# State products of a gated linear attention on the four quarters of the matmul array, one PSUM bank per chunk

## Chip, cores and metric

One core of a Trainium2 chip. The metric is the device time of one execution in microseconds (us), as the median of a set's runs.

## The reference, cut to what matters

```python
# gateloop, B=4, H=8, S=768, D=48; then y is reshaped to (3072, 384) and goes through a maxout FFN
for t in range(S):
    new_re = ar * S_re - ai * S_im              # complex decay of the state
    new_im = ar * S_im + ai * S_re
    kv = np.einsum('bhd,bhe->bhde', k[:, :, t], v[:, :, t])
    S_re, S_im = (new_re + kv, new_im)
    y[:, :, t] = np.einsum('bhd,bhde->bhe', q[:, :, t], S_re)
h = np.maximum(np.maximum(x @ w1, x @ w2), x @ w3)   # 384 -> 768, three times
out = h @ w_out                                       # 768 -> 384
```

Everything is float32.

## The kernel before

A tile `x` is 128 tokens of one batch entry, made of two chunks of 64 tokens. There are 24 tiles; a group `g` is two of them. For each head, a tile needs the contribution of its tokens to the state, K^T V for each chunk ("dk"): 112 columns of the stationary operand (48 cosines in columns 0 to 47, 48 sines in columns 64 to 111, 16 zero columns between) times 48 values. The kernel did it with one matmul per head, for both chunks at once, by keeping v in a block-shaped buffer whose other half is zero:

```python
vbs = [const.tile([P, 2, H // 2, P], FP, ...)]   # [token, chunk, head pair, 2 x 48 (+32)]; token half h is loaded into chunk h, the rest stays 0

def both(t, h):                                  # a head's cosines and sines, 112 columns
    return t[:, h].rearrange("p u d -> p (u d)")[:, 0:DD]

def state(x):
    ...
    ps = psS.tile([P, 2, 512], FP, tag="s", name="dk")
    for h in range(H):
        o = h % 2 * (P - D)
        nc.tensor.matmul(out=ps[0:DD, h // HU, h % HU * 96:h % HU * 96 + 96],
                         lhsT=both(T["Uk", x], h),                  # 128 tokens x 112
                         rhs=T["v", x][:, :, h // 2, o:o + D], ...) # 128 tokens x (2 chunks x 48)
    dk = ps[0:DD, :, 0:HU * 96].rearrange("p a (b c d) -> p a b c d", b=HU, c=2)
    for c in ...:                                                   # VectorE: G_new = G * f + dk
        nc.vector.tensor_tensor(out=new, in0=heads(G[0:DD, c]), in1=f, op=OP.mult)
        nc.vector.tensor_tensor(out=new, in0=new, in1=dk[:, :, :, c], op=OP.add)
```

Other names in the profile: A and B are the score products (64 columns of weights, two column tiles), y the output products (32 columns, four column tiles), F the decay products (48 columns), tp transposes, up and op the FFN. The steps of the stages are listed in an order, and a scheduler then places each instruction on its engine:

```python
def tile_steps(x):
    tr, ct, pr = front(x + 1)          # tr: transposes, ct: F and its exponentials f, pr: VectorE products
    return [call(scores, x, "A"), call(gather, x, "A"), call(scores, x, "B")] + tr[:1] \
        + [call(gather, x, "B"), call(state, x)] + tr[1:] + ct + pr[:1] + kt \
        + [call(outputs, x, tokens(x))] + pr[1:]
```

In the first 113 us the float32 weights are also built from a wider stored form, a chain that goes back and forth between VectorE and ScalarE ("ex", "raw", "wo").

## Time and profile before

| | before |
|---|---|
| median | 742.48 us (742.40 to 744.02, 3 runs) |
| span of the profiled run | 740.5 us |
| TensorE busy | 91%, 7620 matmul records |
| VectorE, ScalarE busy | 70%, 54% |
| one dk stage in the steady part | 1.56 us, 24 of them in all |

The prediction below shows the lines. How to read them: a busy share is an average over stages, so it's cut into windows; the chain of work that ended last then tells, stage after stage, how long the next stage had to wait for this one. Matmul records come two per float32 matmul.

### The profile page before, as it was taken

To read this page: it belongs to the slowest core of one execution; us is meant where nothing else is said; L and a number is where in the kernel's file an instruction comes from. 1 tells how busy PE (TensorE), PEld (TensorE's weight loads), DVE (VectorE), ACT (ScalarE), POOL (GpSimd) and SP (SyncE) were. 2 spreads that over 40 slices of the span, in tenths; PEclk is the share of its full clock that TensorE was granted. 3 is DMA by queue.
4 is the path that set the end of the run, shared out by engine and by line. 5 is a ranking of instruction groups with operands and counts; after the bars stand their busy time and mean duration, and the time that the engine had idled before them with its cause. 6 is when DMAs were issued, how large, how long until landed. Compare 5 with 4: busy or idle time off the path is not lost.

```text
span 740.5 us, 17637 instructions
## 1 busy us (share of the span) xinstructions
PE 670.2 (91%) x7620; PEld 540.8 (73%) x7620; DVE 521.2 (70%) x718; ACT 400.8 (54%) x677; POOL 117.1 (16%) x121
## 2 busy tenths in 40 slices
PE   1266779789999999999999999999999999999998
PEld 0055668578778878878878778778778778778785
DVE  5999998897857867767757767767767677565210
ACT  6778655567556566466466466466475465322000
POOL 9200000403104004004005005004004004000000
PEclk9687799999999999999999999999999999999999
DMA  9780432140410410410410410410410210000000
GB/s 220 212 187 12 107 108 45 30 91 12 85 35 10 89 34 9 91 34 12 86 34 12 86 34 12 86 34 13 86 34 13 44 34 2 1 23 2 12 12 22
DMA packets 134158, 38.91 MB, mean 53 GB/s; under 512 B 126784, under 2 KB 129856, under 8 KB 134080
## 3 DMA queue, kind: packets, MB, share of 16 engines
q1 hardware_dynamic: 133824, 37.76, 23.0%
q8 instruction: 60, 0.98, 0.6%
q14 instruction: 18, 0.15, 0.1%
q10 hardware_dynamic: 256, 0.01, 0.0%
HBM read 33.03 MB, written 4.72 MB: 51 GB/s over the span
## 4 chain that ended last, share of the span: by engine, by line
PE 71%; issue 13%; DVE 7%; ACT 6%; DMA 1%; POOL 1%; SPq 0%; ACTq 0%; POOLq 0%; DVEq 0%
PE up L589 34%; PE op L600 12%; PE tp L442 5%; PE dk L539 4%; PE B L502 4%; PE y L567 3%; PE A L502 3%; ACT e L106 2%; PE mds L405 2%; PE cs L360 2%; PE sfx L405 2%; PE F L455 2%; ACT L L106 1%; ACT w L106 1%; PE cs L362 1%
## 5 line engine op out<-in xcount | busy, mean ns | idle before, releaser
L589 PE MATMUL up<-xT,w 128*128 128x256 f32 (+1 forms) x1404 | 297.5, 365 | 6.7 <-ACT xT L575 6.6
L589 PEld LDWEIGHTS up<-xT,w 128*128 128x128 f32 x1404 | 247.5, 190 | 46.2 <-ACT xT L575 8.9
L600 PE MATMUL op<-wo,hT 128*128 128x384 f32 x288 | 98.9, 492 | 7.3 <-DVE wo L292 3.9
L338 POOL TENSOR_TENSOR ai<-ai,L 128x768 f32<-128x768 f32 x10 | 25.8, 2578 | 382.4 <-ACT L L106 309.0
L600 PEld LDWEIGHTS op<-wo,hT 128*128 128x128 f32 x288 | 52.9, 191 | 41.5 <-issue 4.3
L594 DVE TENSOR_TENSOR hT<-hT,up 128x512 f32<-128x512 f32 (+1 forms) x78 | 49.8, 640 | 40.2 <-PE up L589 40.1
L469 DVE TENSOR_TENSOR Q<-Q,f 112x512 f32<-112x512 f32 x48 | 41.2, 857 | 42.0 <-ACT f L106 42.0
L444 ACT COPY K<-tp 112x512 f32<-112x512 f32 x48 | 27.9, 582 | 61.1 <-PE tp L442 61.0
L592 ACT COPY hT<-up 128x512 f32<-128x512 f32 (+1 forms) x39 | 21.4, 548 | 69.4 <-PE up L589 69.4
L602 ACT COPY ot<-op 128x384 f32<-128x384 f32 x24 | 11.5, 479 | 86.5 <-PE op L600 86.5
L551 DVE TENSOR_TENSOR g<-g,dk 112x384 f32<-112x384 f32 x40 | 22.1, 552 | 47.9 <-PE dk L539 47.4
L567 PEld LDWEIGHTS y<-atm,vb 128*32 128x32 f32 x1536 | 39.3, 111 | 13.9 <-issue 7.9
L539 PEld LDWEIGHTS dk<-vb,uk 128*112 128x112 f32 x384 | 42.0, 180 | 6.8 <-issue 2.5
L567 PE MATMUL y<-atm,vb 128*32 128x64 f32 x1536 | 46.6, 223 | 0.4 <-DVE atm L520 0.4
L567 PE MATMUL y<-QG,g 112*32 112x64 f32 x1536 | 46.0, 221 | 0.0
L469 DVE TENSOR_TENSOR QB<-Q,f 112x512 f32<-112x512 f32 (+1 forms) x48 | 45.4, 982 | 0.0
L539 PE MATMUL dk<-vb,uk 128*112 128x96 f32 x384 | 42.4, 264 | 3.1 <-issue 2.3
L502 PE MATMUL B<-QB,KB 112*64 112x96 f32 x768 | 37.8, 252 | 7.3 <-DVE QB L469 7.3
L502 PEld LDWEIGHTS B<-QB,KB 112*64 112x64 f32 x768 | 33.8, 140 | 11.5 <-issue 10.9
L405 PE MATMUL mds<-Ln,mid 128*128 128x384 f32 x48 | 23.9, 582 | 20.1 <-POOL cuts L120 15.9
L106 ACT ACTIVATE f<-F 48x296 f32<-48x296 f32 x96 | 39.6, 413 | 1.4 <-PE F L455 0.2
L502 PE MATMUL A<-Q,K 112*64 112x96 f32 x768 | 37.7, 249 | 2.6 <-DVE Q L469 2.4
(111 smaller groups left out, 1111.9 us busy)
## 6 DMA issues: line engine op xcount, KB each, us to landing
ar<-in_a_re_dram SPq DMA_DIRECT2D x24, 192.0 KB, 3.7
ai<-in_a_im_dram SPq DMA_DIRECT2D x24, 192.0 KB, 3.9
k<-in_k_dram SPq DMA_DIRECT2D x24, 192.0 KB, 2.9
q<-in_q_dram SPq DMA_DIRECT2D x24, 192.0 KB, 3.0
vb<-in_v_dram SPq DMA_DIRECT2D x96, 48.0 KB, 2.4
out_dram<-ot SPq DMA_DIRECT2D x24, 192.0 KB, 1.9
raw<-in_moe_w_dram SPq DMA_DIRECT2D x5, 768.0 KB, 6.5
raw<-in_moe_w_out_dram SPq DMA_DIRECT2D x3, 768.0 KB, 4.4
```

The costliest lines, as they stand in the source:

```text
L106: tab(nc.scalar.activation(**kw))
L338: (nc.gpsimd if g > 1 else nc.vector).tensor_tensor(out=ai, in0=ai, in1=L, op=OP.mult)
L405: nc.tensor.matmul(out=ps, lhsT=mat, rhs=T["Ln", g][:, c * DM:(c + 1) * DM], start=True, stop=True)
L442: nc.tensor.transpose(out=tp[0:DD, j], in_=both(T["U" + nm, x], hg * HU + j), identity=ident)
L444: nc.scalar.copy(out=T["K", x][0:DD, hs], in_=tp[0:DD])
L469: nc.vector.tensor_tensor(out=out, in0=in_, in1=f.to_broadcast([DD, H, 2 * n, 8]), op=OP.mult)
L502: nc.tensor.matmul(out=ps[o:o + L64, h // HU, h % HU * 96:h % HU * 96 + 96], lhsT=K[0:DD, h, o:o + L64], rhs=Q[0:DD, 2 * h + c], start=Tru ...
L539: nc.tensor.matmul(out=ps[0:DD, h // HU, h % HU * 96:h % HU * 96 + 96], lhsT=both(T["Uk", x], h), rhs=T["v", x][:, :, h // 2, o:o + D], st ...
L567: nc.tensor.matmul(out=y[32 * (r % 4):32 * (r % 4) + 32, r // 4, c * L64:(c + 1) * L64], lhsT=V[:, c, i, lo:lo + 32] if new else G[0:DD, c ...
L589: nc.tensor.matmul(out=ps[:, j], lhsT=ws[i][:, d, f * P:(f + 1) * P], rhs=xT[:, d], start=(d == 0), stop=(d == KD - 1))
L594: nc.vector.tensor_tensor(out=dst, in0=dst, in1=ps, op=OP.max)
L600: nc.tensor.matmul(out=ps, lhsT=hT[:, f, o:o + P], rhs=wo[:, f], start=(f == 0), stop=(f == KF - 1))
```

## The change

The intent: a product of two chunks in one matmul multiplies as many zeros as values. The array can act as four quarters of 64 rows by 64 columns. So a chunk's 64 tokens take half of the rows, a head's cosines or its sines half of the columns, and the four small products of a head run side by side. Each chunk gets its own PSUM bank; the prediction says why.

```diff
         for h in range(H):
             o = h % 2 * (P - D)
-            nc.tensor.matmul(out=ps[0:DD, h // HU, h % HU * 96:h % HU * 96 + 96],
-                             lhsT=both(T["Uk", x], h),
-                             rhs=T["v", x][:, :, h // 2, o:o + D], start=True, stop=True)
-        dk = ps[0:DD, :, 0:HU * 96].rearrange("p a (b c d) -> p a b c d", b=HU, c=2)
+            for lo, hi in ((0, L64), (L64, DD)):
+                for c in range(2):
+                    r = slice(c * L64, (c + 1) * L64)
+                    nc.tensor.matmul(out=ps[lo:hi, c, h * D:(h + 1) * D], lhsT=both(T["Uk", x], h)[r, lo:hi],
+                                     rhs=T["v", x][r, c, h // 2, o:o + D], start=True, stop=True)
+        dk = ps[0:DD, :, 0:DM].rearrange("p c (i u d) -> p c i u d", u=2, d=D)
 ...
-                nc.vector.tensor_copy(out=new, in_=dk[:, :, :, c])
+                nc.vector.tensor_copy(out=new, in_=dk[:, c])
 ...
-            nc.vector.tensor_tensor(out=new, in0=new, in1=dk[:, :, :, c], op=OP.add)
+            nc.vector.tensor_tensor(out=new, in0=new, in1=dk[:, c], op=OP.add)
```

## The prediction

> **What bounds the kernel now.** I read the page's busy shares first, then the table by windows, then the waits of TensorE alone, and last the chain of work that ended last. The shares say where to look, not what the bound is:
>
> ```profile
> PE 670.2 (91%) x7620; PEld 540.8 (73%) x7620; DVE 521.2 (70%) x718; ACT 400.8 (54%) x677; POOL 117.1 (16%) x121
> ```
>
> TensorE leads, but an average over 740 us hides stages, so I cut the span into windows. Columns of the table: the window, its length, busy time (instructions) of PE, PEld, DVE, ACT and POOL, then granted clock, DMA share and GB/s.
>
> ```profile
> 50.00:100.00 50.00, 35.69 (x426) 30.42 (x424) 48.01 (x73) 33.65 (x53) 1.03 (x1) 0.80 0.38 93
> 100.00:150.00 50.00, 41.33 (x571) 32.25 (x573) 42.34 (x59) 29.09 (x50) 8.97 (x6) 0.97 0.23 53
> ...
> 261.10:316.24 55.14, 54.33 (x629) 44.09 (x628) 40.17 (x52) 31.56 (x53) 9.57 (x6) 1.00 0.22 45
> ```
>
> There are two regimes. Until about 190 us VectorE is nearly full (48.0 of 50 us) while TensorE idles. From about 206 us the kernel repeats with a period of about 55.1 us, one group of two 128-token tiles each, and TensorE is busy for 54.3 us of it; VectorE has 15 us to spare, ScalarE 23. The waits of TensorE between 200 and 700 us confirm it (columns: total, times, longest, in us):
>
> ```profile
> PE up L589 <- ACT xT L575: 6.0, 8, 0.8
> PE A L502 <- issue: 0.2, 1, 0.2
> ```
>
> So in the steady part a microsecond taken from TensorE is a microsecond of time, once per tile. The chain of one such group (start, duration in us, line, instructions), where durations run from the end of one stage to the end of the next:
>
> ```profile
> 333.61 2.59 PE up L589 x12
> 336.20 1.56 PE dk L539 x16
> 337.76 2.62 PE up L589 x12
> ...
> 345.98 1.95 PE y L567 x116
> ...
> 361.06 1.47 PE A L502 x32
> 362.53 1.32 PE B L502 x32
> ```
>
> The reader should see the stage to be changed, dk, between two stages that use the whole array, and A, B and y, which already split it by columns. They are the only evidence in this profile of what a split costs and gains. The 1.56 us of dk is 16 instructions (8 heads, each fp32 matmul in two passes) at 97.5 ns. Streaming doesn't set that pace: up streams 256 columns in 2.59 us / 12 = 216 ns, or 0.84 ns a column, so dk's 96 columns need 81 ns. Its 112-column weight load does: 97.5 / 112 = 0.87 ns a column.
>
> **What the Trainium skill says.**
> - "TensorE: Matmul & The Clock Gate", section "LDWEIGHTS (loading the stationary operand)": the load takes columns / 1.2 ns, whatever the rows. For 112 columns that is 93 ns; the trace's 97.5 ns per pass agrees, about 4 ns over.
> - "TensorEngine Tiling (Array Packing)", section "Key Properties": tiles load and multiply in parallel, but changing the tiling mode drains the engine. Both are in the trace: A passes 32 instructions in 1.47 us, 46 ns each, half of one tile's 81 ns stream; and a switch costs time, worked out below.
> - "PSUM — Partial Sum Buffer", section "PSUM bank collisions raise a hardware error": tiles of different rows must not write one bank at once. This is why the change gives each chunk its own bank. No run so far has row tiles.
> - The first page again, section "Wait — 56ns, not 53.3ns?": start to start never below about 25 ns. The trace differs: y's chain entry counts 116 matmul records in 1.95 us; the code issues 128 (some records are missing), which makes 15.2 ns each over four column tiles. The measurement decides.
>
> **The change part by part.**
> *Removed:* per tile 8 matmuls (16 passes) of 128x112 weights by 96 columns, 1.56 us. Half of that product is wasted: each token half multiplies 48 columns of zeros in the block-shaped v.
> *Added:* per tile 32 matmuls (64 passes, 64 loads), each 64 rows by 64 or 48 weight columns by 48 moving columns. The four quarters of a head are issued in turn. If they run side by side, each quarter sees 16 passes. One pass there is the longer of its stream, 48 x 0.84 = 40 ns, and its load, 64 x 0.87 = 56 ns (42 ns for the 48-column quarter). So the load still binds: 16 x 56 = 0.90 us. The issue is a second bound nearby: 64 matmuls at y's 15.2 ns = 0.97 us. I take 0.94 us.
> *Added, hidden in the intent:* two mode switches per tile. The instruction order of both builds shows that in the steady part dk's neighbours don't change: op or up before, tp or up after, all full-array. Entering: A after up takes 1.47 us, the equal B right after A 1.32, so 0.15 us. Leaving: in the same chain up takes 2.79 us after B and 2.59 otherwise, 0.20 us; tp after B 1.02 against 0.87, 0.15 us. One visit thus costs 0.15 + (0.15 or 0.20), about 0.33 us.
> *Unchanged:* VectorE reads the same 112x384 values per half (552 ns each), now from one bank; transfers and evacuations are the same.
> *Sum per tile:* 0.94 + 0.33 = 1.27 us against 1.56 us plus the 0.03 us that up loses after dk on half of the visits, about 1.58: **0.31 us less**.
> *Where it counts:* the dk stages at 206 us and later, two in each of nine groups and one at 697.7 us, are 19. The first five, at 56, 96 to 98, 124, 152 and about 172 us, lie in the stretch whose chain runs through VectorE. There I count nothing. The new order even cuts some of the early stages up (one around an up step, one around transposes), which adds switches in time that TensorE has idle. 19 x 0.31 = 5.9 us. From 742.5 us that is **736.5 us**, 0.8% less.
>
> Does ScalarE take it back? In each group TensorE waits 0.8 us for the copy xT, at the end of a ScalarE stretch that starts when sfx has been multiplied (chain: 323.39 sfx, ScalarE 324.13 to 328.22). sfx comes after dk on TensorE, so that stretch starts earlier with it, and nothing else in it is new. I expect the 0.8 us to stay and the gain to pass through.
>
> **Rivals.**
> 1. *Quarters that differ in rows alone don't overlap*, so only two column tiles run side by side. Then 32 x 56 = 1.80 us + 0.33 = 2.13, 0.55 us more than now, 19 x 0.55 = +10 us: 753. For it: only column tiles are seen running together here. Against it: the skill's tiling page calls all tiles independent.
> 2. *Issue takes over.* With the skill's 25 ns floor, 64 x 25 = 1.6 + 0.33 = 1.93 us: 19 x 0.35 = +7 us: 749. Against it: y's 15.2 ns.
> 3. *The switch is cheaper or is hidden* by the row split, or loads of the two column widths decouple so that a pass costs nearer its stream. 0.90 us with no switch saves 0.68 x 19 = 13 us: 730. For it: nothing in this profile; A, F and y all show the switch.
> 4. *Another engine becomes the bound.* VectorE works 40 of 55 us, ScalarE 32; losing 0.6 us per group can't make them binding. It would give 742.
>
> **Range and chances.** My working gives 736.5. Between a pace of 50 ns a pass with 21 stages that count (saving 0.45 x 21 = 9 us) and 1.1 us a stage with 17 (0.15 x 17 = 2.5 us) lies 733 to 740; with the runs' own spread (742.4 to 744.0) and a little for rivals 1 and 2, I say 731.5 to 741.5. Over 2% faster means below 727.6 us, or 0.78 us less in each of 19 stages: more than rival 3 gives, 3%. Over 2% slower means above 757.3, 0.78 us more in each: more than rival 1, or quarters that hardly overlap: 4%. Within 2%: 93%.
>
> **What would show each step right or wrong.** In the profile after: dk should have 4 times the instructions (1536 matmul records in place of 384), and its chain entry should be about 1.05 to 1.15 us for 64 passes, the entry switch included; up after dk should rise from 2.62 to about 2.79, tp from 0.87 to about 1.02; the group's period should fall from 55.1 to about 54.5 us; the waits for xT should stay at 0.8 us. A dk entry near 2 us means rival 1, near 1.7 us rival 2, near 0.9 with up at 2.6 rival 3. If dk shrinks as said and the period doesn't, rival 4. The prediction is wrong if row tiles behave unlike column tiles, in load or in output, which no trace here shows.

## The result and the profile after

The changed kernel took 739.91 us (738.74 to 741.61, 4 runs) where the kernel before took 742.44 us (742.17 to 744.02, 4 runs). The ratio is 0.9963, with a 95% interval of 0.9939 to 0.9988. The gain is 0.4%, about 2.5 us, where 5.9 us had been forecast.

First the steady part, in the chain of the changed kernel (start, duration, line, instructions; some records are missing, so 57 or 58 stand for 64):

```profile
317.43 1.06 PE dk L544 x58
318.49 1.02 PE tp L442 x8
...
337.36 1.07 PE dk L544 x57
338.42 2.79 PE up L593 x12
```

The dk entry fell from 1.56 to 1.06 us, and the next stage pays for the switch back: 1.02 us for tp, 2.79 us for up. Those are the three figures that the prediction gave. From the first dk of the steady part to the last, 18 visits later, the chain of before goes from 205.96 to 697.68 us, 491.72 us; that of the changed kernel from 208.49 to 694.46 us, 485.97 us. That is 5.75 us, or 0.32 us a visit. Hardly anything took it back: TensorE's waits between 200 and 700 us add up to 6.6 us, where they were 6.2 us. One visit no longer waits for xT and waits 0.9 us at A instead; that group took 54.79 us, the others about 54.47 (columns: total, times, longest).

```profile
PE up L593 <- ACT xT L579: 5.7, 7, 0.8
PE A L502 <- issue: 0.9, 1, 0.9
```

So the steady part did what was forecast. But its first dk starts at 208.49 us, 2.53 us later than before. In this profile the loss is all ahead of the steady part. Following equal instructions of VectorE through both traces, they agree within 0.4 us up to about 107.5 us but for one stage that is ahead at 58 us; then one step of the weight chain comes 1.3 us late, and from 119 us on it's 2.5 to 2.7 us. Here is that place on ScalarE in the timeline of before (start, duration, engine, line, what, and in brackets the idle time ahead of it with what ended it):

```profile
106.72 0.94 ACT L285 ACTIVATE ex<-ex,biases 128x768 int32<-128x768 int32 x1 [1.85 <-DVE ex L284]
107.56 1.67 ACT L106 ACTIVATE f<-F 48x296 f32<-48x296 f32 x4
```

And in the changed kernel:

```profile
106.58 1.69 ACT L106 ACTIVATE f<-F 48x296 f32<-48x296 f32 x4 [1.82 <-PE F L455]
108.30 0.93 ACT L285 ACTIVATE ex<-ex,biases 128x768 int32<-128x768 int32 x1
```

The scheduler has turned two steps around: the four exponentials f, which need F from TensorE, now stand ahead of ex, which VectorE waits for. Nothing in the diff says so; a dk stage of another make-up in tile 1, ahead of this place, was enough (run only1 below). VectorE bounds this stretch, and its timeline shows the wait, first in before, then in the changed kernel:

```profile
107.94 0.95 DVE L286 SCALAR_TENSOR_TENSOR ex<-raw,ex 128x768 int32<-128x768 int32 x1
...
109.26 0.96 DVE L286 SCALAR_TENSOR_TENSOR ex<-raw,ex 128x768 int32<-128x768 int32 x1 [1.16 <-ACT ex L285]
```

The other 1.2 us come a little later. TensorE now waits 2.1 us for the first input of A (1.05 us before), and the step op behind that runs at a lowered clock: its first four matmul records take 2.93 us, where they took 1.56. Behind them is up, for which hT of VectorE then waits, again in before and in the changed kernel:

```profile
119.20 0.41 DVE L594 TENSOR_TENSOR hT<-hT,up 128x256 f32<-128x256 f32 x1
...
121.70 0.42 DVE L598 TENSOR_TENSOR hT<-hT,up 128x256 f32<-128x256 f32 x1 [1.13 <-PE up L593]
```

The window table, before and then changed (window, length, busy times of PE, PEld, DVE, ACT, POOL, then the granted clock as a mean over the window, DMA share and GB/s):

```profile
103.50:107.00 3.50, 3.41 (x21) 2.16 (x22) 3.49 (x6) 1.20 (x2) 0.00 (x0) 0.70 0.52 200
...
113.50:118.00 4.50, 4.36 (x37) 3.35 (x37) 4.50 (x5) 1.19 (x3) 0.00 (x0) 1.00 0.60 130
...
103.50:107.00 3.50, 3.50 (x21) 2.10 (x22) 3.29 (x6) 1.34 (x2) 0.00 (x0) 0.64 0.52 188
...
113.50:118.00 4.50, 4.24 (x28) 2.44 (x30) 4.50 (x6) 0.30 (x1) 0.00 (x0) 0.64 0.22 33
```

So the clock was 0.70 and 1.00 in before, 0.64 and 0.64 in the changed kernel.

### The profile page after: what moved, and what is told of

Its sections match the earlier page's. It is cut to its first block, busy times and chain, and to the rows that moved or that the text cites. A ratio compares the mean times of both kernels' runs of the same rounds, so it can differ in the third digit from the quotient of the medians.

```text
span 737.0 us, 19905 instructions
## 1 busy us (share of the span) xinstructions
PE 664.8 (90%) x8772; PEld 526.1 (71%) x8772; DVE 520.6 (71%) x718; ACT 401.4 (54%) x677; POOL 119.0 (16%) x121
## 3 DMA queue, kind: packets, MB, share of 16 engines
q8 instruction: 69, 1.13, 0.7%
## 4 chain that ended last, share of the span: by engine, by line
PE 69%; issue 17%; ACT 6%; DVE 5%; DMA 1%; POOL 1%; SPq 0%; POOLq 0%; ACTq 0%; DVEq 0%
PE up L593 33%; PE op L604 12%; PE tp L442 5%; PE B L502 4%; PE y L571 3%; PE dk L544 3%; PE A L502 2%; PE mds L405 2%; ACT e L106 2%; PE cs L360 2%; PE F L455 2%; PE sfx L405 2%; ACT L L106 1%; ACT w L106 1%; DMA w<-in_moe_w_dram 1%
## 5 line engine op out<-in xcount | busy, mean ns | idle before, releaser
L604 PE MATMUL op<-wo,hT 128*128 128x384 f32 x288 | 100.4, 498 | 6.6 <-DVE wo L292 3.9
L502 PEld LDWEIGHTS A<-Q,K 112*64 112x64 f32 x768 | 33.1, 138 | 11.2 <-issue 6.0
L571 PEld LDWEIGHTS y<-QG,g 112*32 112x32 f32 x1536 | 40.0, 111 | 0.5 <-issue 0.5
```

The lines of the kernel that those rows point to most:

```text
L502: nc.tensor.matmul(out=ps[o:o + L64, h // HU, h % HU * 96:h % HU * 96 + 96], lhsT=K[0:DD, h, o:o + L64], rhs=Q[0:DD, 2 * h + c], start=Tru ...
L571: nc.tensor.matmul(out=y[32 * (r % 4):32 * (r % 4) + 32, r // 4, c * L64:(c + 1) * L64], lhsT=V[:, c, i, lo:lo + 32] if new else G[0:DD, c ...
L604: nc.tensor.matmul(out=ps, lhsT=hT[:, f, o:o + P], rhs=wo[:, f], start=(f == 0), stop=(f == KF - 1))
```

## The experiments

**Theory (start).** The quarters are worth what was forecast in the steady part. The early loss isn't theirs; it comes from the order on ScalarE that the scheduler picked once tile 1's dk looked different, and from the clock of TensorE. **Rivals:** the loss belongs to the quarters (extra mode switches, stages cut in two) and is spread over the kernel; or it is chance.

### Control: the changed kernel again

> Control, the changed kernel unaltered, in the same rounds as the other three. Theory (start): the steady part gains 5.8 us as predicted (dk entries 1.06 us, period 54.5 us), and some 2.5 to 2.7 us are lost before 122 us, half of it because four exponentials of ScalarE now stand ahead of a weight-rounding step, half because the longer idle time of TensorE lets its clock fall to half for one op step. Then about 739.9 us again. Rival (chance): the first four runs were unlucky and the mean moves towards 737.

Measured: 739.96 us (6 runs, 738.22 to 741.48), ratio 0.9957 (0.9941 to 0.9973). The loss isn't bad luck of the first four runs.

### Quarters only where VectorE doesn't bound: late5

```diff
-        for h in range(H): ...quarters...
+        if x >= 5:
+            for h in range(H): ...quarters...
+        else:
+            for h in range(H): ...one matmul per head, as before...
```

The order of the steps of every engine is then that of before.

> Quarters in tiles 5 to 23 only, the old form in tiles 0 to 4; every engine's order is then that of the kernel before. Theory (start): nothing is lost early, the 19 steady stages gain 5.8 us: 736.6 us against 742.4. Rival (the loss belongs to the quarters themselves, spread over the kernel, or is chance): no better than the changed kernel, 739.9.

Measured: 736.13 us, ratio 0.9903 (0.9889 to 0.9917), against 0.9957 for the changed kernel in the same rounds. Five stages fewer are changed, and it's 4 us faster. In its chain the first steady dk starts at 206.20 us, as in before:

```profile
206.20 1.06 PE dk L545 x58
```

The last starts at 691.84 us, 485.64 us later. The rival that spreads the loss falls.

### Quarters in tile 1 alone: only1

```diff
+        if x == 1:
             ...quarters...
+        else:
+            ...as before...
```

> Quarters in tile 1 alone. Theory (start): this one stage is what reorders ScalarE; it saves a few tenths of TensorE time where TensorE is idle anyway, and costs 1.3 us for the order and up to 1.4 us more if the clock falls: 743.7 to 745.1 us. Rival (the order is harmless): 742.4 or a little less.

Measured: 747.42 us, ratio 1.0058 (1.0041 to 1.0075): 4 us slower than before, more than the 1.3 to 2.7 us expected. One stage of 24, which saves TensorE a few tenths of a microsecond, costs 4 us. The order of its ScalarE steps differs from before in just this place (f ahead of ex, and one copy K two places later), that of TensorE in one (y begun before op). In its profile TensorE's clock was 0.50 from 104 to 108 us and ex of VectorE started at 111.40 us after a wait of 2.30 us for ScalarE.

### The full change with one ordering edge: ordered

```diff
-        nc.scalar.activation(out=ex, in_=ex, func=AF.Relu, scale=8.0, bias=wbias)
+        T["rounding"] = nc.scalar.activation(out=ex, in_=ex, func=AF.Relu, scale=8.0, bias=wbias)
 ...
+                if x == 2:   # f of tile 2 stays behind the rounding step
+                    tc.add_manual_dep(ins.ins, T["rounding"].ins.name, order, reason="rounding first")
```

> The changed kernel in full, with one added ordering edge: the four exponentials f of tile 2 stay behind the rounding step ex on ScalarE, as before. Theory (start): the 1.3 us come back for certain, and with them the shorter idle time of TensorE, so that its clock stays up: 736.6 to 738.5 us. Rival (the loss comes from the extra mode switches and the split stages, which this kernel keeps): 739.9.

Measured: 735.75 us (5 runs, 734.81 to 736.48), a little below the expected range, ratio 0.9899 (0.9884 to 0.9914) against 0.9957 (0.9941 to 0.9973) for the changed kernel in the same rounds. All 24 stages keep their quarters, their extra switches and their cuts, and the loss is gone with one edge that isn't even waited for by a semaphore:

```profile
106.60 0.94 ACT L287 ACTIVATE ex<-ex,biases 128x768 int32<-128x768 int32 x1 [1.94 <-DVE ex L286]
107.44 1.67 ACT L106 ACTIVATE f<-F 48x296 f32<-48x296 f32 x4
...
107.82 0.95 DVE L288 SCALAR_TENSOR_TENSOR ex<-raw,ex 128x768 int32<-128x768 int32 x1
```

Compared step by step, the two traces have the same order on every engine, this one exchange apart. The changed kernel's other new places (y begun inside op at 108 us, one copy K of ScalarE at 101 us, a dk stage cut in three at 154 us, a few steps of VectorE, ScalarE and GpSimd between 125 and 145 us) are all still there, so they are not what cost the time; the exchange is. The gain of 1.0% is the forecast one and a little more.

### Columns alone and rows alone: cols5 and rows5

Both split tiles 5 to 23 only, so that the start stays as before. A second control went with them.

```diff
 # cols5: 128 rows, two column halves          # rows5: two row halves, 112 columns, a bank per chunk
-                for c in range(2): ...          -            for lo, hi in ((0, L64), (L64, DD)):
+  lhsT=both(T["Uk", x], h)[:, lo:hi]            +  lhsT=both(T["Uk", x], h)[r]
+  rhs=T["v", x][:, :, h // 2, o:o + D]          +  rhs=T["v", x][r, c, h // 2, o:o + D]
```

> Control in the same rounds as the next three: quarters in tiles 5 to 23, again about 0.990 of the kernel before, 736 us where that takes 743.

> As late5, but tiles 5 to 23 are split by columns alone: 32 passes of 128 rows, 96 moving columns with their zeros, two tiles side by side. Theory (a pass takes the longer of its stream and its load, tiles overlap, a visit costs two switches): 32 passes at 41 ns as in A, 1.32 + 0.15 us, so a dk entry of 1.47 us, the next up at 2.79 us; a visit costs 1.65 against 1.58 us: 19 x 0.07 = 1.3 us slower than before, about 744.5 where before takes 743. Rival (the column split alone carries the gain): as fast as late5.

> As late5, but split by rows alone: 32 passes of 64 rows, 112 weight columns, 48 moving columns, one bank per chunk. Theory: the 112-column load still takes 98 ns, two row tiles side by side, 16 x 98 = 1.57 + 0.15 us, a dk entry of 1.72 us; a visit costs 1.90 against 1.58: 19 x 0.32 = 6 us slower than before, 749 where before takes 743. Rival (row tiles don't load side by side): a dk entry of 3.3 us and some 773 us. Second rival (fewer rows load or stream faster): a dk entry below 1.56 us.

Measured: late5_again 737.43 us, ratio 0.9919 (0.9899 to 0.9938); cols5 743.44 us, 1.0002 (0.9984 to 1.0020), so in time no different from before; rows5 748.69 us, 1.0077 (1.0058 to 1.0096).

A warning from late5_again's profile. No step before its first steady dk differs from before, in form or in order, and yet that dk starts 2.71 us later than before's 205.96:

```profile
208.67 1.06 PE dk L545 x58
```

So the 2.53 us that the first two profiles showed lie within what single profiles of an unchanged start differ by. That the new order costs time rests on the sets of runs, and on the waits inside the traces, not on these two start times.

The chains, of cols5:

```profile
336.88 1.46 PE dk L543 x31
338.34 2.79 PE up L600 x12
```

and of rows5:

```profile
340.04 1.71 PE dk L544 x32
341.75 2.79 PE up L600 x12
```

Expected were 1.47 and 1.72 us. From the first to the last steady dk cols5 needs 492.82 us and rows5 497.18 us, against 491.72 of before: +0.06 and +0.30 us a visit, where +0.07 and +0.32 had been worked out. So the model of a pass holds for each half of the split by itself: columns alone shorten the load but leave the zeros to stream, rows alone drop the zeros but leave the 112-column load, and either pays the switches. Only both together win.

### One switch fewer: nextf5

```diff
-            + [call(gather, x, "B"), call(state, x)] + tr[1:] + ct + ...
+            + [call(gather, x, "B")] + tr[1:] + [call(state, x)] + ct + ...   # from tile 5 on
```

> As late5, but from tile 5 on dk is issued behind the second transposes, right ahead of F, which is split by columns too. Theory (each change of the array's mode costs 0.15 to 0.2 us, whatever the two modes): one visit to the full array between dk and F falls away in 18 tiles, 0.15 to 0.2 us each: 2.7 to 3.6 us less than late5, about 733 where late5 takes 736. Rival (a switch from one split to another costs as much as two, or the later G makes y wait): no gain over late5.

Measured: 733.03 us, ratio 0.9869 (0.9846 to 0.9891), against 0.9919 for late5_again in the same rounds: 0.5%, 3.7 us. The chain:

```profile
335.77 2.59 PE up L601 x12
338.37 1.07 PE dk L545 x57
339.43 0.65 PE F L455 x16
```

F takes 0.65 us behind dk as it did behind tp, so going from one split to another costs what going from the full array costs, no more. The switch back to the full array between them is gone: the chain from the first to the last steady dk is 481.78 us.

### The clock of TensorE: after_third, filled, best

One more control, a kernel that fills TensorE's second idle time, and one that joins what helped.

> Control, the changed kernel again in the same rounds: about 0.996 of the kernel before. In its profile the granted clock between 114 and 118 us is again near 0.6.

Measured: 737.66 us (735.94 to 739.06), ratio 0.9934 (0.9919 to 0.9948), better than the 0.996 that I had expected. And the profiled run, the fastest, contradicts what I expected of it. The order on ScalarE is the bad one, and yet little is lost:

```profile
105.16 1.69 ACT L106 ACTIVATE f<-F 48x296 f32<-48x296 f32 x4 [0.95 <-PE F L455]
106.88 0.94 ACT L285 ACTIVATE ex<-ex,biases 128x768 int32<-128x768 int32 x1
```

Here f started 1.4 us earlier than in the first profile, since F had run at full clock. The window table of this run has 1.00 where the first profile had 0.64:

```profile
103.50:107.00 3.50, 2.94 (x45) 1.46 (x44) 3.39 (x6) 2.49 (x6) 0.00 (x0) 1.00 0.34 135
```

VectorE's ex started at 107.84 us, about as in before. A part of that was luck: VectorE came to this place 0.55 us earlier than in before and lost 0.46 us of it here, waiting 0.37 us for ScalarE. So the theory needed one more part. The bad order makes ScalarE, and through it VectorE, wait for F; how long depends on the clock that TensorE happens to have there. It has just waited for a weight to be finished, in the timelines of before, of the changed kernel and of this third profile in turn:

```profile
103.59 1.61 PE L600 MATMUL op<-wo,hT 128*128 128x384 f32 x4 [3.85 <-DVE wo L292]
```
```profile
103.47 1.90 PE L604 MATMUL op<-wo,hT 128*128 128x384 f32 x4 [3.90 <-DVE wo L292]
```
```profile
102.94 1.53 PE L604 MATMUL op<-wo,hT 128*128 128x384 f32 x4 [3.50 <-DVE wo L292]
```

The Trainium skill, page "TensorE: Matmul & The Clock Gate", section "What's actually happening", says that the clock falls to half after at least one idle window of about 3.4 us, and that the window runs freely, so that where it falls differs from run to run. These waits are just on that edge, and the runs agree: after waits of 3.90, 4.13, 3.50 and 3.82 us the granted clock from 103.5 to 107 us was 0.64, 0.51, 1.00 and 0.66 in the four profiles of the changed kernel, and 0.70 in before after 3.85 us. The length alone doesn't decide: filled fell to 0.50 after 3.55 us, ordered kept 1.00 after 3.67 us. Before loses nothing there, because ex stood ahead of f. Nor do kernels that have its order or the mended one: nextf5 and best had clocks of 0.62 and 0.53 in this window, and their ex on VectorE started at 107.85 and 107.86 us.

> The changed kernel with two useless matmuls of 512 columns (1.7 us in all at full clock) in TensorE's idle time ahead of A of tile 2; ScalarE keeps the order f ahead of ex. Theory (two parts of the early loss): the granted clock stays at 1.0 in the op step behind, which gives back the 1.3 us that its halving cost and leaves the other 1.3 us: about 738.6 where the changed kernel takes 739.9. Rival (the clock falls with the longer wait as such, or the 1.3 us are hidden): the same as the changed kernel or slower by the filler's own time.

Measured: 738.53 us, ratio 0.9941 (0.9925 to 0.9956), no better than the control's 0.9934. In its profile the second fall of the clock is gone as intended (1.00 from 113.5 to 118 us), but the first stage was slow in that run (0.50, ex on VectorE at 110.43 us), and the filler takes its own time; two steps of VectorE also changed places. So its time tells nothing about the size of the second part. Its trace does, in the table under warm. For the larger loss I had filled the wrong gap.

> Everything that helped in one kernel: quarters in all tiles, the ordering edge for tile 2, and from tile 5 on dk right ahead of F. Theory: as fast as nextf5 or a few tenths faster, 0.986 to 0.987 of the kernel before: 732.5 to 733.5 where before takes 743.

Measured: 733.54 us (4 runs, 733.21 to 733.88), ratio 0.9878 (0.9865 to 0.9890). As fast as nextf5 within the intervals, and with less spread in these four runs.

### Keeping TensorE awake in the first gap: warm

```diff
         ps = psS.tile([P, 2, 512], FP, tag="s", name=nm)
+        for _ in range(14 if x == 2 and nm == "A" else 0):      # useless; in columns that A doesn't use
+            nc.tensor.matmul(out=ps[:, 0, 384:512], lhsT=every, rhs=every, start=True, stop=True)
```

The scheduler put them into the wait at 100 us and left every other step where the changed kernel has it.

> Control, the changed kernel in the rounds of the next run: 737.5 to 740 us, 0.993 to 0.997 of the kernel before, with a spread of some 3 us between its own runs, since the clock of TensorE at F of tile 2 differs from run to run.

> The changed kernel with 14 useless 128-column matmuls (3.0 us at full clock) in TensorE's wait of 3.5 to 3.9 us between 99.6 and 103.5 us, and with every other instruction where the changed kernel has it, ScalarE's f ahead of ex too. Theory (the new order makes ScalarE wait for F, and costs time only where F runs at a lowered clock after that wait): the granted clock from 103.5 to 107 us is 1.00, F ends near 105.1 us in place of 106.5, the early loss is gone: 735.5 to 736.5 us, 0.990 to 0.992 of before, with little spread. Rival (the order costs 1.3 us at any clock, or the early loss is something else): no better than the control.

Measured: after_fourth 739.28 us, ratio 0.9943 (0.9926 to 0.9960); warm 736.89 us (736.23 to 738.82), ratio 0.9917 (0.9899 to 0.9936). With work that does nothing the mean is 0.26%, 1.9 us, lower, but the intervals overlap, so the gain in time isn't clear of noise. Its timeline and window table:

```profile
98.54 3.39 PE L500 MATMUL A<-every 128*128 128x128 f32 x28 [0.95 <-DVE atm L522]
...
103.15 0.72 PE L455 MATMUL F<-cuts,Ln 128*48 128x74 f32 x16
```
```profile
103.50:107.00 3.50, 2.97 (x42) 1.57 (x38) 2.87 (x5) 2.99 (x6) 0.00 (x0) 1.00 0.02 6
```

F ran at full clock. In this profile the step ex of VectorE fell back by 0.54 us against before from the step ahead of it (it had come 1.88 us early, it started 1.34 us early), where the control's fell back by 1.18 us. The early lead isn't the filler's: it was 2.2 us already at 86 us. The other part of the loss is there too: the clock was 0.76 from 113.5 to 118 us. The small spread that I expected did not come.

Put side by side, the fifteen kept traces settle what the times leave open. The columns: the order on ScalarE; the clock from 103.5 to 107 us; from the start of the step ahead (g) to the start of ex on VectorE; the first four matmul records of op behind the wait for A; the wait of VectorE's hT for up.

| trace | first on ScalarE | clock | g to ex, us | op, us | hT waits, us |
|---|---|---|---|---|---|
| after_third | f | 1.00 | 0.92 | 1.56 | 0 |
| warm | f | 1.00 | 1.01 | 2.80 | 1.15 |
| after_fourth | f | 0.66 | 1.64 | 2.68 | 1.15 |
| changed, first | f | 0.64 | 1.70 | 2.93 | 1.13 |
| after_again | f | 0.51 | 2.23 | 2.40 | 1.35 |
| filled | f | 0.50 | 2.79 | 1.56 | 0 |
| only1 | f | 0.50 | 2.85 | 2.93 | 1.21 |
| the eight others | ex | 0.50 to 1.00 | 0.46 to 0.47 | 1.56 | 0 |

With ex first the clock didn't matter at this place. With f first it cost about 0.5 us even at full clock, and up to 2.4 us at half clock. The second part was lost only where op ran slowly, and filled had none of it. How often op runs slowly is left to chance here: TensorE waited 2.0 to 2.6 us for A in all rows with f first but filled, and after_third, with 2.17 us, kept its clock.

| kernel | median us | runs | ratio to before, same rounds | 95% interval |
|---|---|---|---|---|
| changed, first | 739.91 | 4 | 0.9963 | 0.9939 to 0.9988 |
| after_again | 739.96 | 6 | 0.9957 | 0.9941 to 0.9973 |
| late5 | 736.13 | 4 | 0.9903 | 0.9889 to 0.9917 |
| only1 | 747.42 | 6 | 1.0058 | 1.0041 to 1.0075 |
| ordered | 735.75 | 5 | 0.9899 | 0.9884 to 0.9914 |
| late5_again | 737.43 | 6 | 0.9919 | 0.9899 to 0.9938 |
| cols5 | 743.44 | 6 | 1.0002 | 0.9984 to 1.0020 |
| rows5 | 748.69 | 6 | 1.0077 | 1.0058 to 1.0096 |
| nextf5 | 733.03 | 6 | 0.9869 | 0.9846 to 0.9891 |
| after_third | 737.66 | 6 | 0.9934 | 0.9919 to 0.9948 |
| filled | 738.53 | 6 | 0.9941 | 0.9925 to 0.9956 |
| best | 733.54 | 4 | 0.9878 | 0.9865 to 0.9890 |
| after_fourth | 739.28 | 6 | 0.9943 | 0.9926 to 0.9960 |
| warm | 736.89 | 6 | 0.9917 | 0.9899 to 0.9936 |

All of them gave correct results. The median of before was 742.3 to 743.3 us in these rounds.

## Why the prediction was right and wrong

- **The bound of the steady part: right.** TensorE was the bound from 206 us on, and what dk lost came out as time, 5.75 us over 18 visits.
- **The pace of a pass: right, and in fact a little better than taken.** The load of 64 columns sets it. (The prediction's 46 ns for A had the switch in it; the 41 ns of B, 1.32 us / 32, are half of the 81 ns stream.) In the single records of the changed trace the 64-column quarters start a pass every 58 ns and the 48-column quarters every 45 ns. 16 passes of 57 ns make the 0.91 us that remain of the 1.06 us entry when the switch is taken off; I had put 0.94.
- **The two switches: right.** 0.15 or 0.20 us out, read from the next stage; 0.15 us in, with which the dk entries of this kernel, of cols5 and of rows5 all add up.
- **Issue and overlap of row tiles (rivals 1 and 2): ruled out.** 64 matmuls passed in 0.91 us, 14 ns each, and rows5 shows row tiles loading side by side.
- **ScalarE and the wait for xT: right.** The waits stayed at 0.8 us, but for the one visit that waited at A instead.
- **"The first five [...] There I count nothing": wrong, and this is where the gain was lost.** The measured value of that term is about +2.5 us in the first profile, where it should have been 0; in the runs it is the 0.6% between the changed kernel and ordered in the same rounds, 4.2 us. The premise was right, VectorE bounds that stretch; the conclusion, that TensorE's stages can't matter there, wasn't. The prediction says that "the new order even cuts some of the early stages up [...] which adds switches in time that TensorE has idle". It read the new order of TensorE and did not read that of ScalarE, which was on view as well and had f and ex turned around. In its place the runs show: the new order hangs VectorE's weight chain on F, which TensorE computes right after a wait of 3.5 to 4.1 us, often at a lowered clock. That cost 1.2 us at ex in the first profile, and 0.5 to 2.4 us in the others with this order. Behind TensorE's next wait, for A, the clock fell once more in five traces of seven, another 1.1 to 1.4 us. In the profile of after_third the sum was 0, since VectorE came early and the clock stayed up. With the order mended (ordered), the ratio is 0.9899, 7.5 us; the forecast of 5.9 us would have been a ratio of 0.992.
- **What stays open.** How the scheduler came to turn f and ex around wasn't studied. No run undid the second part alone in a way that showed in the time; it is shown in traces. Further falls of the clock exist (in after_fourth it was 0.50 from 148 to 152 us, at cs, and its first steady dk came at 210.66 us). Of the eight traces without the bad order, the three whose clock stayed at 1.00 from 143 to 152 us had their first steady dk at 205.7 to 206.2 us, the five others at 206.3 to 208.7. So part of the spread of all these kernels, before included, is likely the same, which is argued and not shown.

## What to carry to other kernels

Splitting the array paid here because the weight load set the pace and both dimensions shrank; work out a pass as the longer of load and stream, add a switch in and a switch out, and put split stages next to each other. When a scheduler places the instructions, compare the new order on every engine, not only on the one that the change touches: here one changed stage of 24 made the kernel 4 us slower. And where the matmul engine has just idled long enough for its clock to fall, as after the waits of 3.5 us and more here, avoid letting the bounding engine wait for its next result.

## What the Trainium skill lacked or had wrong

- "TensorE: Matmul & The Clock Gate", section "Wait — 56ns, not 53.3ns?", puts the least distance of two matmuls at about 25 ns, without exempting tiles side by side (Part 3 of the same page does, with starts about 4 ns apart). With tiles side by side it was 15.2 ns for y in four column tiles and 14 ns for dk in four quarters.
- "TensorEngine Tiling (Array Packing)", section "Key Properties", says that a change of mode drains the engine, but gives no cost. Measured: 0.15 us going into a split and 0.15 to 0.20 us going back to the full array; from one split to another no more than from the full array (F 0.65 us behind tp and behind dk).
- The same page has no float32 figure for row and column tiles used at once. Here the quarters ran side by side with passes 58 ns (64 columns) and 45 ns (48 columns) apart, about 5 ns above the columns / 1.2 that the first of these pages gives for the load.
- "TensorE: Matmul & The Clock Gate" counts a clock fall in TensorE's own time and doesn't say how it spreads to an engine that waits for the result. Here waits of 3.5 to 4.1 us left the granted clock of the next 3.5 us at 0.51 to 1.00 between runs of one kernel, and VectorE lost 0.5 us at full clock and 1.2 to 1.8 us below it in the same step.
